# Filler matmuls before the last softmax's transposes, and P*V of two head groups ahead of a transpose

## The chip, the cores and the metric

The kernel runs on one core of one Trainium2 chip. The metric is device time in microseconds (us) of one execution. All times "at 366.71" are us from the start of the profiled span. Single profiled runs without rounds are used only for the order of events inside them. Unless it is said otherwise, a time inside an execution is from one profiled execution.

## The reference

Grouped-query attention over a cache, with projections before and after. There are 32 batches of 4 query tokens, 32 query heads on 4 key/value head groups, 2048 cached positions, head size 128:

```python
q = (x @ wq) -> (B, Hq, Sq, Dh)
scores = einsum(q, repeat(k_cache)) * Dh ** -0.5
p = softmax(scores)
out = einsum(p, repeat(v_cache)) -> (B, Sq, Hq * Dh) @ wo
```

K and V are 2 MB each per batch, so 134 of the 151 MB that are read (a transfer is 2048 KB of 1024 bytes).

## The kernel before

The kernel makes one list of operations for each engine, in program order; an operation names the events that it waits for. In the profile PE is the matmul engine, PEld its weight loads, DVE is VectorE, ACT is ScalarE, and L296 is line 296 of the kernel. PE makes the scores of this batch, transposes K of the next one, then makes P*V of the batch two behind, then transposes P; its products land in PSUM, part of which (`ps_r`) this kernel uses as four buffers in turn. In the loop the loads of K and V set the pace: DMA is 59% of the chain that ended last (K 52%, V 7%), and the DMA engines are busy to nine tenths or more in nearly every slice of the page. The end of the program, where nothing is left to load but V of the last batches, is where the change acts. L is the last batch, 31.

```python
for i in range(B):
    pe_qk(i)                       # scores into ps_s, 16 matmuls 128x512
    softmax_max(i)                 # VectorE
    if i >= 3:
        pe_ot(i - 3); ot_evac(i - 3)   # transpose of the finished o_sb, copied by ScalarE
    # ... fills: transposes of K of batch i + 1, and softmax_exp(i) on ScalarE
    softmax_rinv(i)
    if i >= 2:
        pe_pv(i - 2)               # P*V, 64 matmuls
        o_evac(i - 2)
    if i == L:                     # the last P is scaled by 1/sum here
        p.op("dve", ... P_sb[:, :] * rinv[:, L] ..., [("rinv", L)], ("pn", L))
    for f in range(2):
        pe_pt(i, f, ("pn", L) if i == L else ("exp", i))   # 8 transposes of P
        evac_pt(i, f)              # VectorE copy

pe_ot(L - 2); ot_evac(L - 2)
pe_pv(L - 1); o_evac(L - 1)
# ...
def pv_last(g):                    # P*V of one head group of batch L, already transposed
    buf, waits = slot(None)
    for t in range(TV):            # 16 matmuls 128x32
        ... waits + [("v", L, g), ("pt", L, 0), ("pt", L, 1)] ...

pe_ot(L - 1)
ot_evac(L - 1)
pv_last(0)
for g in range(G):
    if g + 1 < G:
        pv_last(g + 1)
    oproj_last(g)                  # 32 matmuls of the output projection
oproj_evac(y_l, n)
```

V of batch L is loaded in four transfers, one for each head group, so that `pv_last(g)` waits for its own quarter only. A matmul is two PE instructions, a weight load and the matmul: the page counts 5927 of each.

Of the kernel before, what the change touches and what calls it, by code (L numbers as in the profile page):

```python
# [56 lines left out]
def bass_standalone__gqa_block_cached__sampling_kernel(  # L57
# [9 lines left out]
    _, G, Sk, Dh = k_cache.shape  # L67
# [24 lines left out]
    with ExitStack() as es:  # L92
        def sbuf(name, shape, dtype):
            return es.enter_context(nc.sbuf_tensor(name, shape, dtype))

        w_sb = sbuf("w_sb", [128, KT, Hq * Dh], BF16)
        wo_sb = w_sb[:, :, :].rearrange("p a (c n) -> p (a c) n", n=D)
# [11 lines left out]
        ident = sbuf("ident", [128, 128], BF16)  # L109
# [13 lines left out]
        p = _Program()  # L123
# [50 lines left out]
        for kt in range(KT):  # L174
            for h in range(Hq):
                p.op("pe", lambda e, kt=kt, h=h: e.matmul(  # L176
                    ps_q(h), lhsT=w_sb[:, kt, h * Dh:(h + 1) * Dh], rhs=xT_sb[:, kt, :],
                    start=(kt == 0 and h % 4 == 0), stop=(kt == KT - 1), skip_group_check=True),
# [15 lines left out]
        def slot(free):  # L194
            n = len(freed)
            freed.append(free)
            return ring[n % NRING], [freed[n - NRING]]
# [3 lines left out]
        def pe_fill(b, f):  # L201
            buf, waits = slot(("kt", b, f))
            buf = slot_of["kt", b, f] = buf.bitcast(BF16)
            for q in range(TB):
                c, v = q // (TB // C), q % (TB // C)
                t = c * TV + f * TB // C + v
                p.op("pe", lambda e, q=q, t=t: e.transpose(  # L207
                    buf[:, q * 128:(q + 1) * 128], K_sb[:, b % NKB, t, :], ident[:, :]),
                    waits + [("k", b), "ident"] if q == 0 else [], ("fill", b, f) if q == TB - 1 else None)

        def evac(b, f):
            buf = slot_of["kt", b, f]
            waits = [("fill", b, f)] + ([("qk", b - 1)] if b else [])
            dst = KT_sb[:, f * TB // C:(f + 1) * TB // C, :, :].rearrange("p v g (r c) -> p (v g) r c", c=C)
            src = buf.rearrange("p (c m r) -> p m r c", c=C, r=R)
            if f in DVE_FILLS:
                p.op("dve", lambda e: e.tensor_copy(dst, src), waits, ("kt", b, f))  # L217
            else:
                p.op("act", lambda e: e.activation(dst, src, ACT.Copy), waits, ("kt", b, f))  # L219

        def pe_pt(i, f, ready):
            buf, waits = slot(("pt", i, f))
            buf = slot_of["pt", i, f] = buf.bitcast(BF16)
            for q in range(8):
                p.op("pe", lambda e, q=q: e.transpose(  # L225
                    buf[:, q * 128:(q + 1) * 128], P_sb[:, (8 * f + q) * 128:(8 * f + q + 1) * 128], ident[:, :]),
                    waits + [ready] if q == 0 else [], ("ptf", i, f) if q == 7 else None)
# [7 lines left out]
        def pe_qk(i):  # L235
            waits = [("kt", i, f) for f in range(NFILL)]
            waits += [("qe", j) for j in range(Hq // 4)] if i == 0 else [("exp", i - 1)]
            for c in range(4):
                for g in range(G):
                    p.op("pe", lambda e, c=c, g=g: e.matmul(  # L240
                        ps_s[32 * g:32 * (g + 1), c * 512:(c + 1) * 512],
                        lhsT=QT_sb[:, i, REP * g:REP * (g + 1), :],
                        rhs=KT_sb[:, 4 * c:4 * (c + 1), g, :],
                        start=True, stop=True, tile_position=(0, 32 * g)),
                        waits, ("qk", i) if (c, g) == (3, G - 1) else None)
# [8 lines left out]
        def pe_pv(i):  # L254
            buf, waits = slot(("o", i))
            slot_of["o", i] = buf
            waits = waits + [("pt", i, 0), ("pt", i, 1), ("v", i)]
            for t in range(TV):
                for g in range(G):
                    pv_mm(buf, i, g, t, waits if t == 0 and g == 0 else [],  # L260
                          ("pv", i) if (t, g) == (TV - 1, G - 1) else None)

        def o_evac(i):
            buf = slot_of["o", i]
            p.op("act", lambda e: e.activation(o_sb[:, :], buf[:, 0:Dh], ACT.Copy, scale=rinv[:, i:i + 1]),  # L265
                 [("pv", i), ("rinv", i)] + ([("oT", i - 1)] if i else []), ("o", i))

        def pe_ot(i):
            buf, waits = slot(("ot", i))
            buf = slot_of["ot", i] = buf.bitcast(BF16)  # L270
            p.op("pe", lambda e: e.transpose(buf[:, 0:128], o_sb[:, :], ident[:, :]), waits + [("o", i)], ("oT", i))  # L271

        def ot_evac(i):
            buf = slot_of["ot", i]
            p.op("act", lambda e: e.activation(  # L275
                oT_sb[:, :, i * Sq:(i + 1) * Sq], buf[:, 0:128].rearrange("p (h s) -> p h s", s=Sq), ACT.Copy),
                [("oT", i)], ("ot", i))

        def softmax_max(i):
            p.op("dve", lambda e: e.tensor_reduce(mx[:, i:i + 1], ps_s[:, :], AX.X, ALU.max), [("qk", i)], ("mx", i))  # L280
            p.op("dve", lambda e: e.tensor_scalar(negmx[:, i:i + 1], mx[:, i:i + 1], -scale, None, op0=ALU.mult),  # L281
                 [("mx", i)], ("negmx", i))

        def softmax_exp(i):
            p.op("act", lambda e: e.activation(  # L285
                P_sb[:, :], ps_s[:, :], ACT.Exp, bias=negmx[:, i:i + 1], scale=scale, accum_out=ssum[:, i:i + 1]),
                [("negmx", i)] + ([("ptf", i - 1, 1)] if i else ["qproj"]), ("exp", i))

        def softmax_rinv(i):
            p.op("dve", lambda e: e.reciprocal(rinv[:, i:i + 1], ssum[:, i:i + 1]), [("exp", i)], ("rinv", i))  # L290
# [12 lines left out]
        def oproj(n):  # L303
            buf, waits = slot(("oe", n))
            oproj_mm(buf, n, range(Hq), waits + [("wo", c) for c in range(4)] + [("ot", OG * n + OG - 1)], ("op", n))
            oproj_evac(buf, n)

        def oproj_evac(buf, n):
            p.op("dve", lambda e: e.tensor_copy(y_sb[:, n, :], buf[:, 0:NC]), [("op", n)], ("oe", n))
# [7 lines left out]
        for f in range(NFILL):  # L317
            pe_fill(0, f)
            evac(0, f)
        L = B - 1  # L320
        for i in range(B):
            pe_qk(i)
            softmax_max(i)
            if i >= 3:
                pe_ot(i - 3)
                ot_evac(i - 3)
                if i > OG and i % OG == 2:
                    oproj(i // OG - 1)
            if i < L:
                for f in (0, 1):  # L330
                    pe_fill(i + 1, f)
                    evac(i + 1, f)
            softmax_exp(i)
            if i < L:
                for f in range(2, NFILL):
                    pe_fill(i + 1, f)
                    evac(i + 1, f)
            softmax_rinv(i)
            if i >= 2:
                pe_pv(i - 2)  # L340
                o_evac(i - 2)
            if i == L:
                p.op("dve", lambda e: e.tensor_scalar(P_sb[:, :], P_sb[:, :], rinv[:, L:L + 1], None, op0=ALU.mult),  # L343
                     [("rinv", L)], ("pn", L))
            for f in range(2):
                pe_pt(i, f, ("pn", L) if i == L else ("exp", i))
                evac_pt(i, f)
# [7 lines left out]
        n = NOG - 1  # L355

        def pv_last(g):
            buf, waits = slot(None)
            for t in range(TV):
                p.op("pe", lambda e, t=t: e.matmul(  # L360
                    buf[:, 0:32], lhsT=V_sb[:, L % NVB, g, t, :], rhs=PT_sb[:, L % 2, t, 32 * g:32 * (g + 1)],
                    start=(t == 0), stop=(t == TV - 1)),
                    waits + [("v", L, g), ("pt", L, 0), ("pt", L, 1)] if t == 0 else [],
                    ("pvl", g) if t == TV - 1 else None)
            p.op("dve", lambda e: e.tensor_copy(
                oT_sb[:, 8 * g:8 * (g + 1), L * Sq:(L + 1) * Sq], buf[:, 0:32].rearrange("p (h s) -> p h s", s=Sq)),
                [("pvl", g)], ("otl", g))

        def oproj_last(g):
            oproj_mm(y_l, n, range(8 * g, 8 * (g + 1)), [("otl", g), ("ot", L - 1), ("exp", L)],  # L370
                     ("op", n) if g == G - 1 else None)

        pe_ot(L - 1)
        ot_evac(L - 1)
        pv_last(0)
        for g in range(G):
            if g + 1 < G:
                pv_last(g + 1)
            oproj_last(g)
        oproj_evac(y_l, n)  # L380
        for m in range(NOG - 1):
            oproj_out(m, ("sp",))
# [57 lines left out]
```

## Time and profile before

| what | value |
|---|---|
| device time, median of 3 runs | 383.13 us (382.86 to 383.46) |
| profiled span | 381.2 us |
| DMA traffic | 400 GB/s mean |
| last score matmul ends, P ready | 361.98, 367.59 |
| PE idle before the transposes of the last P | 3.04 us |
| granted clock 0.5 | 366.71 to 373.54 |
| y (last projection) copied from | 378.24 |

These are lines of the page of the kernel before, with others left out between them. "PEclk" on the profile page below is the granted clock of PE in tenths, in 40 slices of the span; a group line of PE there ends with the idle time of PE just before that group's instructions and what ended most of it.

```profile
span 381.2 us, 12591 instructions
PEclk9999999999788699999999999999999999999978
q8 instruction: 46, 0.75, 0.8%
L296 PE MATMUL ps_r<-w_sb,oT_sb 128*32 128x256 bf16 x384 | 11.9, 273 | 3.8 <-issue 2.6
```

The clock is low in three places in the middle and in the last two slices. The last two lines were on the page all along and I read past them: PE's own instructions come in by DMA, in 46 packets, 0.75 MB (the page doesn't say whose they are; experiments below tie them to PE), and the projections of the earlier batches had stood 2.6 us in all "on issue", that is, with nothing that they waited for.

The windows view of the kernel before gives for each stretch the busy time of PE (and its count of instructions), of its weight loads and of the other engines, then the granted clock, the DMA share and GB/s. The stretches are cut on a grid of 3.413 us, on which all changes of the granted clock in this trace lie (93.65, 100.48, 110.72, 117.54, 124.37, 131.20, 366.71, 373.54 and 380.37).

```profile
363.30:366.71 3.41, 1.08 (x64) 0.90 (x64) 1.25 (x3) 2.17 (x3) 0.00 (x0) 1.00 1.03 410
366.71:370.13 3.42, 2.49 (x41) 2.30 (x45) 2.09 (x4) 0.42 (x2) 0.00 (x0) 0.50 0.66 254
370.13:373.54 3.41, 2.85 (x97) 2.44 (x89) 0.51 (x3) 0.64 (x2) 0.00 (x0) 0.50 0.43 155
373.54:376.95 3.41, 3.41 (x120) 2.87 (x116) 0.38 (x2) 0.00 (x0) 0.00 (x0) 1.00 0.03 6
```

PE is busy for 1.08 of 3.41 us while the last softmax is made; the next two windows run at half clock.

The timeline of PE in the kernel before (start, duration, line, operation, count, and in brackets the idle time ahead of it with what ended it):

```profile
363.52 1.08 PE L248 MATMUL ps_r<-V_sb,PT_sb 128*32 128x128 bf16 x64 [1.39 <-DMA V_sb<-in_v_cache_dram]
367.64 1.89 PE L225 MATMUL ps_r<-ident,P_sb 128*128 128x128 bf16 x16 [3.04 <-DVE P_sb L343]
369.32 0.31 PE L271 MATMUL ps_r<-ident,o_sb 128*128 128x128 bf16 x1
369.57 1.90 PE L248 MATMUL ps_r<-V_sb,PT_sb 128*32 128x128 bf16 x64
372.03 0.27 PE L271 MATMUL ps_r<-ident,o_sb 128*128 128x128 bf16 x1 [0.56 <-ACT o_sb L265]
372.15 1.01 PE L360 MATMUL ps_r<-PT_sb,V_sb 128*128 128x32 bf16 x32
373.10 1.25 PE L296 MATMUL ps_s<-w_sb,oT_sb 128*32 128x256 bf16 x32
374.28 0.56 PE L360 MATMUL ps_r<-PT_sb,V_sb 128*128 128x32 bf16 x16
374.77 1.06 PE L296 MATMUL ps_s<-w_sb,oT_sb 128*32 128x256 bf16 x32
375.76 0.57 PE L360 MATMUL ps_r<-PT_sb,V_sb 128*128 128x32 bf16 x16
376.26 1.93 PE L296 MATMUL ps_s<-w_sb,oT_sb 128*32 128x256 bf16 x64
```

From the top: P*V of batch 29, the idle time, transposes of P (L225), the transpose of batch 29's output, P*V of batch 30, its transpose, P*V of batch L group by group (L360) between the four parts of the projection (L296). From 367.64 PE hardly rests.

### The profile page before, as it was taken

To read this page: it belongs to the slowest core of one execution; us is meant where nothing else is said; L and a number is where in the kernel's file an instruction comes from. 1 tells how busy PE (TensorE), PEld (TensorE's weight loads), DVE (VectorE), ACT (ScalarE), POOL (GpSimd) and SP (SyncE) were. 2 spreads that over 40 slices of the span, in tenths; PEclk is the share of its full clock that TensorE was granted. 3 is DMA by queue.
4 is the path that set the end of the run, shared out by engine and by line. 5 is a ranking of instruction groups with operands and counts; after the bars stand their busy time and mean duration, and the time that the engine had idled before them with its cause. 6 is when DMAs were issued, how large, how long until landed. Compare 5 with 4: busy or idle time off the path is not lost.

```text
span 381.2 us, 12591 instructions
## 1 busy us (share of the span) xinstructions
PE 275.9 (72%) x5927; PEld 224.2 (59%) x5927; DVE 275.0 (72%) x302; ACT 207.6 (54%) x259; POOL 0.7 (0%) x6
## 2 busy tenths in 40 slices
PE   1876778873837578787777677778776778788756
PEld 1875656662726567666555566666555557566645
DVE  0007999994538395889888885989977876899841
ACT  1006777761615562766666664677655646667630
POOL 0000000000000000000000000000000000000000
PEclk9999999999788699999999999999999999999978
DMA  8999999999999999999999999999999999999981
GB/s 328 437 426 420 412 422 410 413 391 411 403 409 412 417 418 420 415 407 417 422 416 413 420 419 412 419 416 417 413 416 420 416 414 420 416 419 410 351 315 32
DMA packets 27251, 152.32 MB, mean 400 GB/s; under 512 B 1472, under 2 KB 1984, under 8 KB 22592
## 3 DMA queue, kind: packets, MB, share of 16 engines
q1 hardware_dynamic: 27104, 151.49, 97.2%
q8 instruction: 46, 0.75, 0.8%
q10 hardware_dynamic: 96, 0.03, 0.0%
q14 instruction: 5, 0.04, 0.0%
HBM read 151.26 MB, written 0.26 MB: 397 GB/s over the span
## 4 chain that ended last, share of the span: by engine, by line
DMA 59%; PE 17%; ACT 11%; DVE 9%; issue 3%; SPq 1%
DMA K_sb<-in_k_cache_dram 52%; DMA V_sb<-in_v_cache_dram 7%; ACT KT_sb L219 6%; ACT P_sb L285 5%; DVE KT_sb L217 5%; PE ps_r L207 4%; PE ps_r L296 3%; DVE mx L280 3%; PE ps_r L248 3%; PE ps_r L225 2%; PE ps_s L240 2%; PE ps_s L296 1%; DVE PT_sb L231 1%; PE ps_r L360 0%; SPq L129 0%
## 5 line engine op out<-in xcount | busy, mean ns | idle before, releaser
L207 PE MATMUL ps_r<-ident,K_sb 128*128 128x128 bf16 x2048 | 138.5, 225 | 63.3 <-DMA K_sb<-in_k_cache_dram 35.5
L217 DVE COPY KT_sb<-ps_r 128x1024 bf16<-128x1024 bf16 x128 | 148.0, 1216 | 32.8 <-PE ps_r L207 32.6
L207 PEld LDWEIGHTS ps_r<-ident,K_sb 128*128 128x128 bf16 x2048 | 121.2, 101 | 79.7 <-DMA K_sb<-in_k_cache_dram 36.2
L219 ACT ACTIVATE KT_sb<-ps_r 128x1024 bf16<-128x1024 bf16 x128 | 124.3, 1025 | 68.0 <-PE ps_r L207 67.9
L280 DVE TENSOR_REDUCE mx<-ps_s 128x1 f32<-128x2048 f32 x32 | 73.3, 2291 | 8.2 <-PE ps_s L240 5.8
L285 ACT ACTIVATE P_sb<-ps_s,negmx 128x2048 bf16<-128x2048 f32 x32 | 63.0, 1969 | 2.2 <-DVE negmx L281 2.1
L231 DVE COPY PT_sb<-ps_r 128x1024 bf16<-128x1024 bf16 x64 | 41.4, 686 | 16.4 <-PE ps_r L225 15.0
L248 PE MATMUL ps_r<-V_sb,PT_sb 128*32 128x128 bf16 x1984 | 34.2, 223 | 15.3 <-ACT KT_sb L219 8.9
L248 PEld LDWEIGHTS ps_r<-V_sb,PT_sb 128*32 128x32 bf16 x1984 | 28.8, 98 | 20.4 <-ACT KT_sb L219 18.4
L275 ACT ACTIVATE oT_sb<-ps_r 128x128 bf16<-128x128 bf16 x31 | 8.6, 277 | 57.2 <-PE ps_r L271 57.2
L225 PE MATMUL ps_r<-ident,P_sb 128*128 128x128 bf16 x512 | 35.1, 223 | 3.7 <-DVE P_sb L343 3.0
L240 PE MATMUL ps_s<-KT_sb,QT_sb 128*32 128x512 bf16 x512 | 34.3, 382 | 4.5 <-DVE KT_sb L217 1.7
L225 PEld LDWEIGHTS ps_r<-ident,P_sb 128*128 128x128 bf16 x512 | 29.4, 99 | 7.3 <-DVE P_sb L343 3.2
L240 PEld LDWEIGHTS ps_s<-KT_sb,QT_sb 128*32 128x32 bf16 x512 | 10.9, 95 | 15.7 <-issue 4.5
L187 DVE CAST QT_sb<-ps_r 128x512 bf16<-128x512 f32 x2 | 1.3, 687 | 22.6 <-PE ps_r L176 22.6
L265 ACT ACTIVATE o_sb<-ps_r,rinv 128x128 bf16<-128x128 f32 x31 | 11.4, 367 | 10.8 <-PE ps_r L248 10.8
L189 ACT ACTIVATE QT_sb<-ps_r 128x512 bf16<-128x512 f32 x2 | 1.1, 594 | 26.1 <-PE ps_r L176 26.1
L176 PE MATMUL ps_s<-P_sb,w_sb 128*128 128x128 bf16 x128 | 9.3, 230 | 7.8 <-DMA w_sb<-in_wq_dram 7.8
L296 PE MATMUL ps_r<-w_sb,oT_sb 128*32 128x256 bf16 x384 | 11.9, 273 | 3.8 <-issue 2.6
L296 PEld LDWEIGHTS ps_r<-w_sb,oT_sb 128*32 128x32 bf16 x384 | 10.1, 97 | 5.1 <-issue 4.0
L176 PEld LDWEIGHTS ps_s<-P_sb,w_sb 128*128 128x128 bf16 x128 | 8.1, 103 | 8.3 <-issue 4.5
L271 PEld LDWEIGHTS ps_r<-ident,o_sb 128*128 128x128 bf16 x31 | 3.0, 98 | 12.9 <-issue 12.9
(26 smaller groups left out, 62.6 us busy)
## 6 DMA issues: line engine op xcount, KB each, us to landing
K_sb<-in_k_cache_dram SPq DMA_DIRECT2D x32, 2048.0 KB, 25.5
V_sb<-in_v_cache_dram SPq DMA_DIRECT2D x31, 2048.0 KB, 27.2
w_sb<-in_wq_dram SPq DMA_DIRECT2D x4, 2048.0 KB, 14.8
w_sb<-in_wo_dram SPq DMA_DIRECT2D x4, 2048.0 KB, 24.1
V_sb<-in_v_cache_dram SPq DMA_DIRECT2D x4, 512.0 KB, 11.0
P_sb<-in_x_dram SPq DMA_DIRECT2D x1, 256.0 KB, 2.7
out_dram<-y_sb SPq DMA_DIRECT2D x14, 16.0 KB, 8.9
out_dram<-y_sb ACTq DMA_DIRECT2D x2, 16.0 KB, 1.6
```

What stands on the lines that cost most here:

```text
L176: p.op("pe", lambda e, kt=kt, h=h: e.matmul(ps_q(h), lhsT=w_sb[:, kt, h * Dh:(h + 1) * Dh], rhs=xT_sb[:, kt, :], start=(kt == 0 and h % 4 ...
L207: p.op("pe", lambda e, q=q, t=t: e.transpose(buf[:, q * 128:(q + 1) * 128], K_sb[:, b % NKB, t, :], ident[:, :]), waits + [("k", b), "iden ...
L217: p.op("dve", lambda e: e.tensor_copy(dst, src), waits, ("kt", b, f))
L219: p.op("act", lambda e: e.activation(dst, src, ACT.Copy), waits, ("kt", b, f))
L225: p.op("pe", lambda e, q=q: e.transpose(buf[:, q * 128:(q + 1) * 128], P_sb[:, (8 * f + q) * 128:(8 * f + q + 1) * 128], ident[:, :]), wai ...
L231: p.op("dve", lambda e: e.tensor_copy(PT_sb[:, i % 2, 8 * f:8 * f + 8, :].rearrange("p t q -> p (t q)"), buf), [("ptf", i, f)] + ([("pv", ...
L240: p.op("pe", lambda e, c=c, g=g: e.matmul(ps_s[32 * g:32 * (g + 1), c * 512:(c + 1) * 512], lhsT=QT_sb[:, i, REP * g:REP * (g + 1), :], rh ...
L248: p.op("pe", lambda e: e.matmul(buf[32 * g:32 * (g + 1), 0:Dh], lhsT=PT_sb[:, i % 2, t, 32 * g:32 * (g + 1)], rhs=V_sb[:, i % NVB, g, t, : ...
L265: p.op("act", lambda e: e.activation(o_sb[:, :], buf[:, 0:Dh], ACT.Copy, scale=rinv[:, i:i + 1]), [("pv", i), ("rinv", i)] + ([("oT", i - ...
L280: p.op("dve", lambda e: e.tensor_reduce(mx[:, i:i + 1], ps_s[:, :], AX.X, ALU.max), [("qk", i)], ("mx", i))
L285: p.op("act", lambda e: e.activation(P_sb[:, :], ps_s[:, :], ACT.Exp, bias=negmx[:, i:i + 1], scale=scale, accum_out=ssum[:, i:i + 1]), [( ...
L296: p.op("pe", lambda e, h=h, j=j: e.matmul(buf[32 * j:32 * (j + 1), 0:NC], lhsT=oT_sb[:, h, 32 * n:32 * (n + 1)], rhs=wo_sb[:, h, NC * j:NC ...
```

## The change

Its intent is to keep PE busy while the last P is made, so that the clock stays up, and to start P*V of the last batch while ScalarE still copies the output of the batch in front.

```diff
+        def pe_idle(n):
+
+            buf, waits = slot("idle")
+            for k in range(n):
+                p.op("pe", lambda e: e.matmul(buf, lhsT=ident[:, :], rhs=wo_sb[:, 0, 0:512], start=True, stop=True),
+                     waits + [("wo", 0)] if k == 0 else [], "idle" if k == n - 1 else None)
 ...
             if i == L:
+                pe_idle(12)
                 p.op("dve", ...
 ...
-        pe_ot(L - 1)
-        ot_evac(L - 1)
-        pv_last(0)
-        for g in range(G):
-            if g + 1 < G:
-                pv_last(g + 1)
-            oproj_last(g)
+        pv_last(0)
+        pv_last(1)
+        pe_ot(L - 1)
+        ot_evac(L - 1)
+        oproj_last(0)
+        pv_last(2)
+        oproj_last(1)
+        pv_last(3)
+        oproj_last(2)
+        oproj_last(3)
```

(The slots of `pv_last` also get names, so that a later user of the same buffer waits for them.) The product of the fillers is never read.

More of the change, by code (lines that the diff above doesn't have):

```diff
@@ L357, in pv_last @@
         def pv_last(g):
-            buf, waits = slot(None)
+            buf, waits = slot(("otl", g))
             for t in range(TV):
```

## The prediction

> **What bounds the kernel now.** The page's chain of work that ended last is 59% DMA (52% K loads), at a mean 400 GB/s; no compute engine is over 72% busy. The change leaves that streaming part alone: it acts only on the last 17 us of the 381.2 us span, after the last transposes of K.
>
> **The tail, from the timeline and the chain (us from the span's start).** The scores of the last batch L end at 361.98; max 362.03–364.33, exp 364.54–366.60, reciprocal and scaling end at 367.59. Meanwhile PE has only P*V of batch 29, 363.52–364.60, then idles 3.04 us until 367.64. From 366.71 to 373.54 the granted clock is 0.5 (windows view; 1.0 on both sides). In that stretch 16 transposes of P take 1.89 us (1.07 at full clock, at 359.93), P*V of batch 30 takes 1.90 (1.08 at 358.92), with o_sb and its transpose behind it, P*V of batch L two groups 1.01, and the projection runs 373.10–378.19. y is copied at 378.24, the outputs follow.
>
> **The clock.** [...] all clock changes lie on one 3.413 us grid. I tabulated PE busy time per window of that grid: at full clock those with 1.69 us busy or more stayed full after the start-up; those with 0.00, 0.60 and 1.08 us were followed by half clock. Half clock ended after windows with 2.85 us busy or more, not after 2.49. The window before the last drop has the 1.08.
>
> **What the change adds.** Twelve 128x512 matmuls on data already loaded. A 512-wide pass costs about 0.21 us (an estimate: the score group, four passes side by side, lasts 1.05 us with some 0.2 us drain), so 2.6 us, from 364.6 to about 367.2, just before P is ready at 367.6. They don't delay P and bring the window from 1.08 to about 3.2 us busy, so full clock should hold.
>
> **What that is worth.** At full clock: transposes of P end 368.7 (before 369.5), their DVE copies about 369.6 (370.26), P*V of batch 30 about 369.8 (371.47), its o_sb 370.2 (371.88). Alone this would be worth 1.5 to 2 us. P*V of L itself hardly gains: 16 matmuls of 32 columns take about 0.5 us at either clock.
>
> **What takes some back.** V of the last batch comes in four transfers. By issue time plus time to landing (DMA view) they land at 369.7, 371.1, 372.2 and 373.5, already slow (205 GB/s). Before, PE came later than all. Now group 1 would wait for 371.1, and the new order puts the transpose of batch 30 behind it, although its o_sb is ready at 370.2. So: group 1 371.1–371.6, transpose 371.9, its copy by ACT 372.2, projection from 372.25 instead of 373.10; then the same sequence, 4.9 us instead of 5.1. y is ready about 1.0 us earlier. The reordering by itself I expect to gain nothing, or to cost about 0.5 us against the filler matmuls alone.
>
> **Prediction.** 382.1 us, 8 in 10 between 381.2 and 383.1. Faster by over 2%: 0.01; within 2%: 0.98; slower: 0.01.
>
> **Right if the profile shows:** granted clock 1.0 from 366 to 373; the filler group of about 2.6–2.8 us ending before the transposes of P, still at 367.6; 16 transposes in 1.07; second group of the last P*V waiting on the V transfer; projection starting near 372.2. **Wrong if:** the clock falls all the same (then fillers take 5 us and delay P's transposes by up to 2 us); V lands earlier (gain near 2 us) or later; or run-to-run clock phase makes the mean penalty before differ from the profiled one.

The grid and the table of windows are read from the trace of the kernel before. The median before, 383.13 us, less 1.0 us for the earlier y, is the 382.1 us. The 0.21 us for a 512-wide pass was an estimate; in that trace the 16 score matmuls of batch L start in fours at 360.92, 361.15, 361.37 and 361.58, 0.22 us apart, those of a four within 0.01 us.

## The result, and the profile after

| | before | after |
|---|---|---|
| device time, median | 383.16 us (4 runs) | 383.22 us (4 runs) |
| ratio, 95% interval | | 1.0001 (0.9984 to 1.0018) |
| granted clock 0.5 in the tail | 366.71 to 373.54 | never |
| first projection matmul | 373.10 | 371.99 |
| y copied from | 378.24 | 378.26 |

A ratio is the mean time of one kernel's fast runs over that of the other's fast runs of the same rounds, so it is not quite the ratio of the medians in the table. The time did not move.

The clock did. Two lines of the page after:

```profile
span 381.2 us, 12614 instructions
PEclk9999999998778699999999999999998999999999
```

The windows of the same stretch after:

```profile
363.30:366.71 3.41, 3.16 (x74) 1.99 (x76) 1.21 (x4) 2.29 (x3) 0.00 (x0) 1.00 1.03 410
366.71:370.13 3.42, 2.97 (x100) 2.27 (x97) 2.04 (x3) 0.67 (x3) 0.00 (x0) 1.00 0.66 250
370.13:373.54 3.41, 2.35 (x76) 1.89 (x75) 0.38 (x2) 0.28 (x1) 0.00 (x0) 1.00 0.43 153
```

PE is busy 3.16 us where it was 1.08, and the clock stays at 1.00. The timeline of PE after (one short line, of the transpose of batch 29's output at 368.42, left out):

```profile
363.39 1.08 PE L248 MATMUL ps_r<-V_sb,PT_sb 128*32 128x128 bf16 x64 [1.38 <-DMA V_sb<-in_v_cache_dram]
364.63 2.54 PE L324 MATMUL ps_r<-w_sb,ident 128*128 128x512 bf16 x11 [0.16 <-issue]
367.51 1.07 PE L225 MATMUL ps_r<-ident,P_sb 128*128 128x128 bf16 x16 [0.35 <-DVE P_sb L351]
368.57 1.08 PE L248 MATMUL ps_r<-V_sb,PT_sb 128*32 128x128 bf16 x64
369.75 0.55 PE L368 MATMUL ps_r<-PT_sb,V_sb 128*128 128x32 bf16 x16
370.90 0.56 PE L368 MATMUL ps_r<-PT_sb,V_sb 128*128 128x32 bf16 x16 [0.60 <-DMA V_sb<-in_v_cache_dram]
371.32 0.22 PE L271 MATMUL ps_r<-ident,o_sb 128*128 128x128 bf16 x1
371.99 1.06 PE L296 MATMUL ps_s<-w_sb,oT_sb 128*32 128x256 bf16 x32 [0.46 <-ACT oT_sb L275]
372.98 0.57 PE L368 MATMUL ps_r<-PT_sb,V_sb 128*128 128x32 bf16 x16
373.48 0.40 PE L296 MATMUL ps_s<-w_sb,oT_sb 128*32 128x256 bf16 x7
374.91 0.94 PE L296 MATMUL ps_s<-w_sb,oT_sb 128*32 128x256 bf16 x25 [1.03 <-issue]
375.78 0.56 PE L368 MATMUL ps_r<-PT_sb,V_sb 128*128 128x32 bf16 x16
376.27 1.93 PE L296 MATMUL ps_s<-w_sb,oT_sb 128*32 128x256 bf16 x64
```

(One of the twelve fillers, L324, is missing from the records; its weight load is there.) The projection starts 1.1 us earlier. Then, after the 7th matmul of its second part, PE halts. There is no semaphore between the 7th and the 8th matmul: they belong to one loop and only its first waits. Between the start of the last matmul before the halt (373.60) and that of the next instruction, a weight load (374.91), lie 1.30 us, of which the view counts 1.03 as idle because its record of the matmul in front runs to 373.87. From 375.78 on both kernels do the same work at the same time. From the last part of the chain of waits after (lines left out after the first):

```profile
360.30 10.55 DMA V_sb<-in_v_cache_dram
373.55 0.33 PE ps_s L296 x7
373.87 1.03 issue
374.91 0.94 PE ps_s L296 x25
```

So the question is what "issue" is here.

### The profile page after: what moved, and what is told of

Read it like the earlier page. It is cut to its first block, busy times and chain, and to the rows that moved or that the text cites. A ratio compares the mean times of both kernels' runs of the same rounds, so it can differ in the third digit from the quotient of the medians.

```text
span 381.2 us, 12614 instructions
## 1 busy us (share of the span) xinstructions
PE 278.2 (73%) x5938; PEld 223.9 (59%) x5939; DVE 275.0 (72%) x302; ACT 207.6 (54%) x259; POOL 0.7 (0%) x6
## 4 chain that ended last, share of the span: by engine, by line
DMA 61%; PE 15%; ACT 11%; DVE 9%; issue 3%; SPq 1%
DMA K_sb<-in_k_cache_dram 58%; ACT KT_sb L219 6%; DVE KT_sb L217 5%; ACT P_sb L285 5%; PE ps_r L207 4%; PE ps_r L296 3%; DVE mx L280 3%; DMA V_sb<-in_v_cache_dram 3%; PE ps_r L248 2%; PE ps_s L240 2%; PE ps_r L225 2%; PE ps_s L296 1%; DVE PT_sb L231 1%; SPq L129 0%; PE ps_r L368 0%
## 5 line engine op out<-in xcount | busy, mean ns | idle before, releaser
L248 PEld LDWEIGHTS ps_r<-V_sb,PT_sb 128*32 128x32 bf16 x1984 | 28.0, 97 | 20.1 <-ACT KT_sb L219 18.2
```

What stands on the lines that cost most here:

```text
L248: p.op("pe", lambda e: e.matmul(buf[32 * g:32 * (g + 1), 0:Dh], lhsT=PT_sb[:, i % 2, t, 32 * g:32 * (g + 1)], rhs=V_sb[:, i % NVB, g, t, : ...
```

## The experiments

**The theory.** In the whole trace of the kernel before there are eleven more halts of this kind, of 0.6 to 2.0 us, and counted over PE's records (weight loads, matmuls, waits) they stand at places 3777, 4033, 4289, 4545, 6593, 6849, 7105, 7361, 9409, 9665 and 9921: all 256 or a multiple of it apart. The halt after the change stands at 11713 (with the missing record), again in that series. The queue "q8 instruction" fits the series: it carries 46 packets of 16384 bytes, and the kernel before has 46 places of the series (193, 449 and so on to 11713). Each of its packets starts only after PE has passed one place, and PE passed no next place sooner than 1.27 us after the end of the packet. So I call the places boundaries, and a packet the block of instructions behind the next boundary; that is inferred from these counts and times, the trace names neither. The eleven halts end 1.27 to 1.61 us after their packet has been moved, the halts of the tail in the table below 1.66 to 1.91 us. How long a packet waits is not explained by the load on the DMA engines alone: at 42 of the 44 boundaries ahead of the tail of the kernel before it started 2.3 to 4.2 us after PE had passed, but at 115.04 and 280.99 only 1.03 and 0.45 us after, with K and V streaming no less (386 and 407 GB/s in the windows that hold these two).

The fetch theory is then (its request is inferred, no trace shows it): the tail's last block is asked for when PE passes a boundary at about 369 to 370, but its packet starts only at about 371.85, while V of the last batch is being moved, and PE can't go on past the next boundary before about 374.9. That is a floor under the end of the program, and the kernel before stood just above it, without showing it in the profile above.

**The rivals.** First, the order theory, which the prediction itself had named: the reordering puts the transpose of batch 30 behind the wait for V, and that ate the gain. Second, the halt belongs to a time, a clock state, or to the projection's own operands, and has nothing to do with instruction blocks.

"Pads" below are pairs of a weight load and a 128x32 matmul, 2 PE instructions each, put in where PE waits for K in batches 24 to 30. They are there to shift the block boundaries against the tail. They also take one of the four buffers in each of these seven batches, in all runs with pads alike, and add a little work to the loop:

```python
def pe_pad(i, n):
    buf, waits = slot(("pad", i))
    for k in range(n):
        p.op("pe", lambda e: e.matmul(buf[:, 0:32], lhsT=ident[:, :], rhs=ident[:, 0:32], start=True, stop=True),
             waits if k == 0 else [], ("pad", i) if k == n - 1 else None)
```

A run is called by the number of its heading below; the two runs that repeat 7 and 9 are 13 and 14 and stand under 9. All sets of runs were timed beside the kernel before; its medians in those sets were 383.39, 383.49, 383.16 and 382.97 us.

### 1. The fillers alone

```diff
+                pe_idle(12)          # kept; the end of the program in the order of before
```

> The twelve filler matmuls kept, the order of before restored. Fetch theory (PE halts at a block boundary, 212 PE instructions before its end, until a 16 KB instruction block arrives about 374.9 us, whatever PE did before): the projection starts earlier than in the changed kernel (about 371.5 against 371.99), a longer halt of about 1.5 us stands at the same 7th matmul of the second projection group, and y is copied at 378.2 as before; time within 0.3 us of 383.2. Order theory (the reordering ate the gain of the clock): no halt, y at about 376.5 and 1.5 us faster, 381.7 us.

Measured: 383.58 us, ratio 1.0011 (0.9998 to 1.0023). Two lines of PE's timeline:

```profile
373.07 0.40 PE L296 MATMUL ps_s<-w_sb,oT_sb 128*32 128x256 bf16 x6
375.21 0.94 PE L296 MATMUL ps_s<-w_sb,oT_sb 128*32 128x256 bf16 x26 [1.75 <-issue]
```

The projection started at 371.59, 0.4 us earlier than with the reordering, and the halt was 0.7 us longer, 1.75 us idle against 1.03: it began earlier, and it ended 0.3 us later, at 375.21, after a packet that was moved 0.3 us later. y came at 378.57. The order theory falls as the reason for the lost gain.

### 2. The reordering alone

```diff
-                pe_idle(12)          # removed; the new order kept
```

> The new order without the fillers. Fetch theory: 24 PE instructions fewer, so the boundary falls where it did before (12 matmuls later in the second projection group than in the changed kernel); clock at 0.5 from about 366.7 to 373.5, projection starts at 373.1 to 373.3, hardly any halt, time within 0.3 us of 383.2. Order theory: the order costs about 0.5 us at either clock, 383.7 us.

Measured: 383.22 us, ratio 0.9997 (0.9985 to 1.0009). One expectation missed: the clock was at half for one window only (368.40 to 371.81), so the projection started at 372.50, not 373.1. A halt of 0.44 us idle took it back, and y came at 378.16:

```profile
375.16 0.60 PE L296 MATMUL ps_s<-w_sb,oT_sb 128*32 128x256 bf16 x13 [0.44 <-issue]
```

As expected, it stood 12 matmuls later than in the changed kernel (after the 19th, not the 7th, of the second part), because the 24 instructions of the fillers are missing.

### 3. The change with 21 pads

```diff
+            if 24 <= i < L:
+                pe_pad(i, 3)
```

> The changed kernel with 21 pairs of a weight load and a tiny matmul (42 PE instructions) put in where PE waits for K, in batches 24 to 30, 3 in each. Fetch theory: the boundary moves from 212 to 254 instructions before the end, to the start of the second projection group or just before it; the block still comes at about 374.9, the halt grows to about 1.8 us, y at about 378.8, 0.6 us slower, 383.8 us. A halt that belongs to a time, a clock state, or to the projection's operands stays with the 7th matmul of the second group or at 373.9 us, and the time stays at 383.2.

Measured: 385.35 us, ratio 1.0053 (1.0032 to 1.0073). The profiled run, at 383.64 us, was as expected: the halt moved to the end of the first part of the projection, was 1.53 us idle and ended at 374.73, and y came at 378.90. A halt bound to the operands or to the 7th matmul would not have moved. But the unprofiled runs were up to 2.7 us slower than expected. That was taken up in run 12.

### 4. The change with 70 pads

```diff
+            if 24 <= i < L:
+                pe_pad(i, 10)
```

> The changed kernel with 70 such pairs (140 PE instructions, 10 in each of seven batches). Fetch theory: boundaries 352 and 96 instructions before the end; the first is crossed at about 370.9 with its block there, the block for the last 96 is needed only at about 375.5 and is there by 374.9 to 375; no halt over 0.3 us after 371, y at about 377.0 to 377.3, 1.0 to 1.2 us faster than the changed kernel, 382.0 to 382.3 us. A halt that is not of instruction fetch: no change, 383.2, or slower by the pads.

Measured: 382.20 us, ratio 0.998 (0.9966 to 0.9993); y at 377.34. 140 instructions more, and the kernel is about 1 us faster. One part was missed: a halt of 0.66 us idle remained, at the boundary crossed near 371, one matmul before the end of the first group of the last P*V. It cost little: V of the second group landed at 371.11, and PE went on at 371.23.

### 5. The change without half of the last V (wrong result)

```diff
-                for g in range(G):
+                for g in range(2):       # V of the last two groups of batch L is not loaded
 ...
-                    waits + [("v", L, g), ...
+                    waits + [("v", L, min(g, 1)), ...
```

> The changed kernel without the loads of V of the last two head groups of the last batch (1 MB of 152 MB; the result is wrong on purpose, the old contents of the buffer are used). The PE instruction stream is the same. Theory that the instruction block waits behind V in the DMA engines: PE asks for it at 368.9 as before, but its transfer starts at about 370 instead of 371.8, the block is there by about 373, the halt at the 7th matmul of the second group (1.3 us) shrinks to under 0.3 us, y at about 377.1 and 1.1 us faster than the changed kernel, 382.1 us. If the block does not wait behind V (a fixed delay of the request, or a halt of another kind), the halt stays and the time stays at 383.2 to 383.4.

Measured: 382.23 us, ratio 0.9979 (0.996 to 0.9999); the result is wrong, as meant. PE passed the boundary at 369.04, the packet of 16384 bytes started at 370.05 and not at 371.84, and there was no halt:

```profile
372.29 1.06 PE L296 MATMUL ps_s<-w_sb,oT_sb 128*32 128x256 bf16 x32 [0.46 <-ACT oT_sb L275]
373.28 0.56 PE L368 MATMUL ps_r<-PT_sb,V_sb 128*128 128x32 bf16 x16
373.78 1.06 PE L296 MATMUL ps_s<-w_sb,oT_sb 128*32 128x256 bf16 x32
```

The DMA view shows the packet too: the first line is of this run from 370 to 371 us, the second of the changed kernel from 371 to 372 us, which has none from 370 to 371.

```profile
q8 instruction: 1, 0.02, 7.0%
q8 instruction: 1, 0.02, 8.4%
```

The instruction stream was the same as in the changed kernel, so what delays the block is the data still to be moved. The trace does not say which of the 16 DMA engines carries the packet, so how V holds it up is not shown, only that it starts earlier with less V.

Where the last block stood in the runs so far (times of packets are from the trace's records of that queue; PE passes a boundary with its first weight load or matmul beyond it):

| run | PE passes the boundary before | packet moved | PE goes on past the next |
|---|---|---|---|
| before | 370.40 | 371.87 to 373.22 | 375.12, no halt |
| after | 368.87 | 371.84 to 373.18 | 374.91, halted |
| fillers alone | 369.01 | 372.18 to 373.51 | 375.21, halted |
| reordering alone | 369.96 | 371.90 to 373.25 | 375.16, halted |
| change, 21 pads | 369.16 | 371.92 to 373.06 | 374.72, halted |
| change, half of V | 369.04 | 370.05 to 371.17 | 373.80, no halt |

PE's arrival at the earlier boundary varies by 1.5 us; the start of the packet by only 0.3 us, unless there is less V. In the kernel before, the block was to be had at about 374.9 (an estimate: 373.22 and the 1.7 us that the change showed between packet and going on; the other halts in the table show 1.7 to 1.9), about 0.2 us before PE came.

### 6. Fillers, order of before, 70 pads

> Fillers, order of before, 70 pad pairs. Fetch theory: boundaries 352 and 96 instructions before the end, as in the run of the change with 70 pairs; the block for the last 96 is asked for when the boundary 352 is crossed (about 371) and comes at about 375.7, so y at about 377.3, 382.2 us, the same as that run although the projection starts 0.4 us earlier. Order theory: 0.5 us faster than that run, 381.7.

Measured: 382.38 us (381.33 to 383.8), ratio 0.9977 (0.9958 to 0.9996). The number fits, but the profiled run, one of the slower ones (383.10 us), went another way than expected. A halt in P*V of batch 29 left its window with 1.33 us busy, the clock fell, and the fillers took 4.21 us instead of 2.54 and held the transposes of P up to 369.71. Window, and a line of the timeline:

```profile
362.21:365.62 3.41, 1.33 (x65) 1.07 (x66) 2.37 (x2) 1.25 (x2) 0.00 (x0) 1.00 1.02 401
```

```profile
365.66 4.21 PE L324 MATMUL ps_r<-w_sb,ident 128*128 128x512 bf16 x11 [0.17 <-issue]
```

This is the danger of fillers that the prediction had named, and it makes this run no test of the order.

### 7. Fillers, order of before, 49 pads

```diff
+                pe_idle(12)          # and the order of before
+            if 24 <= i < L:
+                pe_pad(i, 7)
```

> Fillers, order of before, 49 pad pairs (98 instructions), chosen so that the block for the last 310 instructions is asked for at the second filler (364.8) and not during the V tail: boundaries 566, 310 and 54 before the end. Fetch theory: no halt or under 0.3 us at 310, a halt of about 0.7 us at 54 (block there at about 375.8), y at about 376.7, 381.5 us, the fastest of all. If the phase of the blocks does not matter: the same as the fillers alone, 383.5.

Measured: 381.85 us, ratio 0.9956 (0.9943 to 0.997), the fastest of all; again (run 13) 381.56 us, ratio 0.9963 (0.9951 to 0.9975). The packet for the last 310 instructions was moved from 368.67, that for the last 54 from 372.31, and neither was late, so y came a little before the expected 376.7. The end of PE's timeline:

```profile
371.52 1.06 PE L296 MATMUL ps_s<-w_sb,oT_sb 128*32 128x256 bf16 x32
372.51 0.56 PE L376 MATMUL ps_r<-PT_sb,V_sb 128*128 128x32 bf16 x16
373.01 1.06 PE L296 MATMUL ps_s<-w_sb,oT_sb 128*32 128x256 bf16 x32
374.00 0.57 PE L376 MATMUL ps_r<-PT_sb,V_sb 128*128 128x32 bf16 x16
374.49 1.93 PE L296 MATMUL ps_s<-w_sb,oT_sb 128*32 128x256 bf16 x64
```

From the start of the projection to its end (376.42) are 4.9 us without a halt, the length that the prediction had assumed.

### 8. The kernel before with 63 pads

```diff
+            if 24 <= i < L:
+                pe_pad(i, 9)         # no fillers, order of before
```

> The kernel before (no fillers) with 63 pad pairs, so that its boundaries stand as in the run of fillers with 49 pairs (570, 314, 58 before the end). Without the fillers the clock falls to half at about 366.7, so instruction fetch is not the limit: no halt over 0.5 us, the projection from about 373.1, y at 378.2, 383.2 to 383.5 us. If the pads alone, not the removed halt, made the fast runs fast: about 382.

Measured: 382.59 us, ratio 0.9979 (0.9965 to 0.9993). A miss: the pads alone gained 0.8 us by the ratio, 0.9 by the medians, about half of what run 7 gained. In the profiled run the clock was at half for one window (368.15 to 371.57), not two, the projection started at 372.54 and ran without a halt, and y came at 377.49. The expectation had taken the two slow windows of one profile for a constant. In the second profile of before (run 10) there were two again, in run 2 there was one. With one window and the projection from 372.50, run 2 still had y at 378.16, held there by the halt; here nothing held it. How often the kernel before has one slow window or two is not recorded, so how its 0.8 us are made up is not shown.

### 9. The change with 49 pads, and its twin again

> The changed kernel (its new order) with 49 pad pairs, to compare with the fillers in the order of before and the same pads: the reordering by itself, with the halt out of the way. Prediction of record and fetch theory alike: the transpose of batch 30 stands behind V group 1 (landing 371.0), the projection starts at about 372.0 instead of 371.5, y at about 377.0 instead of 376.5, 0.5 us slower than the 381.85 of that run, 382.3 us. If the reordering is free or helps: 381.9 or less.

Measured: 383.11 us (382.18 to 383.61), ratio 0.9995 (0.998 to 1.0009), and no halt. In the profile the projection came 0.6 us later with the new order, as expected (6.04 us from the start of the second group of the last P*V to the copy of y, 5.45 us in run 7). But in that execution V of the second group had also landed later, at 371.93, where the other profiles have 370.86 to 371.55, and the two sets had been run on different chips. So both kernels were run once more:

> The fillers in the order of before with 49 pad pairs, once more, now on the same chip as its twin in the new order. 381.85 us again, 381.5 to 382.2; from the start of the second group of the last P*V to the copy of y 5.45 us, as in its first profile.

> The same pads with the new order. Its first runs came out at 383.11, of which the trace gives the order only 0.6 us (6.04 against 5.45 us from the second group of the last P*V to the copy of y) and the rest to V data that landed some 0.7 us later. If that rest was chance: 382.4 on the same chip as the twin, 0.5 to 0.6 slower than it. If the new order itself makes V late: 1.2 us slower again.

Measured: 381.56 us with the order of before, 382.17 us with the new order, ratios to the kernel before 0.9963 (0.9951 to 0.9975) and 0.998 (0.9963 to 0.9996). The reordering costs about 0.6 us once the halt is out of the way: the intervals overlap, but the profiles show the same (projection from 371.61 and 372.21, y at 376.56 and 377.17). Why V was late in the first set is not known.

### 10 and 11. Both kernels once more

> The kernel before, unchanged, for another profile at another phase of the clock grid. Fetch theory: if the clock is at half for less of the tail than in the first profile, the projection starts sooner and a halt appears, 188 PE instructions before the end, until about 374.9; y between 378.0 and 378.6 whatever the phase. If no such floor exists: y as early as the clock allows, 377.3 with one window of half clock.

382.93 us. The clock was at half from 366.17 to 372.99, two windows again, so this was not the other phase that was wanted. The second part of the projection began 0.2 us earlier than in the first profile, at 374.54, and took 1.24 us instead of 1.06. The timeline of the weight loads shows why:

```profile
375.17 0.33 PEld L296 LDWEIGHTS ps_s<-w_sb,oT_sb 128*32 128x32 bf16 x13 [0.18 <-issue]
```

It is a short halt at the boundary, after the 19th weight load, ending 1.75 us after its packet had been moved (372.08 to 373.42); y came at 378.19. So the kernel before itself meets the floor as soon as it is 0.2 us early.

> The changed kernel, unchanged, for another profile. Fetch theory: the halt again at the 7th matmul of the second projection group, ending about 1.7 us after the end of a 16 KB instruction transfer that starts at 371.8 to 372.2; y at 378.2 to 378.6.

383.14 us. The halt stood at the same place, the packet was moved from 371.99 to 373.32, PE went on at 375.05, y at 378.40. As expected.

### 12. Why 21 pads were so slow

> The change with 21 pad pairs once more, because its unprofiled runs (384.6 to 386.5) were slower than its profiled one (383.6). If the halt of 1.5 us leaves the window of the clock grid that holds it under about 1.7 us busy, the clock falls after it and the last projection groups run at half: 384.5 us or more, granted clock 0.5 in 375 to 379. If a profile at 384.5 us or more shows full clock, it is something else; a profile at 383.6 leaves it open.

385.38 us, so it caught the slow case. Windows and timeline:

```profile
373.42:376.83 3.41, 1.95 (x58) 1.49 (x56) 0.19 (x1) 0.00 (x0) 0.00 (x0) 1.00 0.04 10
376.83:380.24 3.41, 3.41 (x76) 2.60 (x77) 0.19 (x1) 0.00 (x0) 0.00 (x0) 0.50 0.00 0
```

```profile
377.19 3.40 PE L296 MATMUL ps_s<-w_sb,oT_sb 128*32 128x256 bf16 x64
```

The clock fell at 376.83, in the window after the halt, and the last 64 projection matmuls took 3.40 instead of 1.93 us. The course was as expected, a halt and then half clock from the next window on; the rule was not: the window had 1.95 us busy, above the 1.69 us that I had read from the kernel before as enough.

## Why the prediction was wrong

Up to the start of the projection every step held (the after tail runs 0.13 us earlier throughout, from the last scores on):

| step | predicted | measured |
|---|---|---|
| fillers, ending before P is ready | 2.6 us, to 367.2 | 364.40 to 367.17 |
| clock in the tail | 1.0 | 1.00 |
| 16 transposes of P | 1.07 us | 1.07 us |
| group 1 of the last P*V waits for V until | 371.1 | 370.90 |
| projection starts | 372.25 | 371.99 |
| projection with P*V between, to its end | 4.9 us | 6.2 us |
| time | 382.1 us (381.2 to 383.1) | 383.22 us |

The step that failed is "then the same sequence, 4.9 us instead of 5.1". It took PE's instructions for granted. The sequence halted 1.30 us at a boundary of an instruction block, and with that the gain of 1.0 us was gone. The runs showed three things in its place. The halt follows the boundary when pads shift it (runs 3, 4, 7). It goes away when there is less V to move and the packet starts 1.8 us earlier (run 5: 370.05 instead of 371.84). And with the boundaries moved out of the way the same sequence takes 4.9 us and y comes 1.8 us earlier than before (run 7, in the order of before). Run 14, the change itself with 49 pads, did what had been predicted of the change: projection from 372.21, 4.9 us to its end, y at 377.17, 1.1 us earlier than before, and 382.17 us.

That both kernels ended at the same 378.2 is only half a coincidence. In the kernel before, the slow clock brought PE to the boundary about 0.2 us after the block was to be had (the estimate above), so a faster PE could gain only those 0.2 us. And the fillers, 24 instructions ahead of the tail, put the boundary 12 matmuls nearer to its start, so that more work was left behind it: from passing it to the copy of y are 3.12 us before (375.12 to 378.24) and 3.35 us after (374.91 to 378.26). The two cancel. That they cancel so well is luck.

What was right: the fillers hold the clock; the clock is worth something in the tail once the halt is out of the way (run 7 against run 8: the projection starts 1.0 us earlier, the median is 0.7 us lower; this is less than the "1.5 to 2 us" predicted for the clock alone); V of the last groups lands late and the reordering makes PE wait for it. "The reordering by itself I expect to gain nothing, or to cost about 0.5 us" was measured at 0.6 us (runs 13 and 14). "Within 2%" was right and no news.

What was wrong beside the main step: the threshold for the clock. The windows of the kernel before gave "1.69 us busy or more stay at full clock". Windows with 1.33 us (run 6) and even 1.95 us (run 12) were followed by half clock, one with 1.75 us (run 2, 361.58 to 364.99) was not. What weighs beside busy time is left open. In the kernel before, the window from 97.06 to 100.48 held nothing on PE but transposes of K (35 recorded, 3.42 us busy), at half clock, and full clock followed.

## What to carry to other kernels

Idle time of an engine whose bracket says "issue" is worth a look at its place in the engine's own instruction count. If such places are 256 apart, as here, suspect that the engine is waiting for its instructions; then work added in front of a critical stretch, even idle work, moves the boundaries in it. In the loop of the kernel before a block took 2.3 to 4.2 us to start (but for the two above), 1.0 to 1.1 us to be moved and then, at the eleven halts, 1.3 to 1.6 us until PE went on, so a PE that gets through 256 instructions in less than 5 to 7 us can be held up (an estimate: the sum). Before a faster clock or a better order is credited with a gain in the tail of a program, look for what arrives there by DMA whatever the engines do: the last data and the last instructions.
